# Attention into a two-layer product on one core: chunks of 512 tokens that follow the batches, with the left-over tokens gathered into a ninth

## The chip, the core and the metric

One Trainium2 chip, one core of it. The metric is device microseconds of one execution of the whole program, the median of the runs shown. Engines are named as in the profile: PE (TensorE, its weight loads apart as PEld), DVE (VectorE), ACT (ScalarE), POOL (GpSimd) and SP (SyncE, which here only issues DMAs). Each engine takes its instructions strictly in the order of its own queue.

## The reference

Eight batches of 576 tokens, 8 heads of 64. Keys and values are averaged over windows of 8 tokens, so a batch has 72 keys; attention over them gives 4,608 tokens of 512 values, which go through two matrices with a gelu between.

```python
k_p = k.reshape(B, H, Sp, pool, D).mean(axis=3)          # B=8, H=8, S=576, D=64, Sp=72
v_p = v.reshape(B, H, Sp, pool, D).mean(axis=3)
scores = scale * np.matmul(q, k_p.transpose(0, 1, 3, 2))
attn = softmax(scores)
attn_out = np.matmul(attn, v_p).astype(np.float32)
x = attn_out.transpose(0, 2, 1, 3).reshape(B * S, H * D)  # 4608 x 512
h = x @ w_in                                              # 512 x 2048
g = h * (1.0 / (1.0 + np.exp(-1.702 * h)))
out = (g @ w_out).astype(np.float32)                      # 2048 x 512
```

The two weight matrices come as float64.

## The kernel before

**Precision.** Every operand of a large product is split into a rounded part and the exact rest (`hi`, `lo`), and each product is three passes on PE: hi·hi, hi·lo, lo·hi. ACT usually makes the `hi` by a copy and DVE or POOL the `lo` by a subtraction.

**Weights.** They are decoded from float64 in 33 parts (`decode_weights`): ACT scales (L520, L522), DVE puts sign and exponent together (L527, L528), POOL adds (L532), ACT rounds to `hi` (L538), and POOL, or DVE for every fourth part, subtracts (L543). The raw words of a part lie where the part two places on will live.

**Attention.** A batch has two pieces, 256 and 320 tokens. Keys and values are loaded by SP, 64 keys of two heads to a tile, in one buffer that is refilled after DVE's window sum (L147); ACT and PE turn the keys; `score` (L308) gives scores in PSUM, DVE subtracts the maximum (L320, L321), ACT takes the exponential, DVE sums and multiplies (`tail` L381, `main` L389), turns the weights (`mt`, L422) and splits them (`al`, L426), and `weigh` (L452 to L455) makes x transposed: `pav` in PSUM, from which ACT writes `hi` (L458) and DVE `lo` (L459) of x. Batch 0's products of window sums, queries and weights are turned on PE. The work of a batch is a generator whose `yield`s give a chunk that must be through before it goes on.

**Chunks.** The second part takes the 4,608 tokens in chunks: three of 256 and ten of 384, whose borders do not match the batches. Where a piece reaches over the border of a chunk, its later tokens wait in `stage` (L461) and are moved by `unstage` (ACT L466, POOL L467). For each chunk and each 128 of the 2,048 columns (256 for a chunk of 256 tokens), `moe_in` makes h by 12 matmuls (L563 to L565), ACT makes `gh` and `g` (L569, L570), DVE (chunks 0 and 1) or POOL makes `gl` (L572); `moe_out` then adds to the chunk's output tiles of 128 tokens (L583 to L585), which stay in PSUM over the whole chunk. At the end of a chunk ACT copies each tile to `osb` (L588) and issues its DMA (L589); the first tile of a chunk borrows the one buffer of tag `g`, the others take the two of tag `osb`.

**Order.** The main loop goes through the steps (a chunk and a block of columns). Between steps it pumps the attention's generator: PACE = 5 stages a step, with EARLY = 13 ahead, as far as x has a free buffer of two. DECODED = 0.8 parts of weights are decoded per pumped stage. SP's loads stand where the program issues them: `fetch_batch(b + 1)` in piece 0 of batch b. Within these data dependencies a scheduler of the compiler puts each engine's queue in order, so the queue can differ from the program's order.

PSUM: three banks for output tiles (`ps_o`), two for h (`ps_h`), three for attention (`ps_a`).

## Time and profile before

| | |
|---|---|
| runs | 1000.5, 997.71, 998.65 us; median 998.65 |
| span of the profiled execution | 994.9 us; its own device time is not listed, and 3.75 us of the median lie outside this span |
| first product of chunk 0, of the third chunk (token 512) | 41.8 us, 185.5 us |
| first product of the last chunk | 920.8 us |
| last matmul ends | 990.3 us |
| DMA bytes | 47.2 MB read, 9.4 MB written |

Busy time is each engine's own, over the whole span; PE's large share comes from the second part, and the first 200 us look different from the rest. In rows of the profile the third and later columns of a group are busy time, mean ns of one instruction, and the engine's idle time ahead of it with what ended it.

### The profile page before, as it was taken

What the parts mean: (1) busy time and instruction counts of PE and PEld (TensorE: products, weight loads), DVE (VectorE), ACT (ScalarE), POOL (GpSimd) and SP (SyncE); (2) the same over time, 40 slices, a digit from 0 to 9 for tenths busy, and PEclk for the clock granted to TensorE, in tenths of its full rate; (3) what the DMA queues carried; (4) which work ended last, traced back from release to release, by engine and by line L of the source; (5) the groups of instructions that cost most, each with busy time, mean ns of one, the idle gap of its engine ahead of it and who ended that gap; (6) DMA issues with size and microseconds to landing.
All of it is one profiled execution on the core that took longest, in us unless ns stands there. A gap on an engine that the chain in (4) does not pass through costs nothing.

```text
span 994.9 us, 13412 instructions
## 1 busy us (share of the span) xinstructions
PE 939.4 (94%) x4957; PEld 835.0 (84%) x4957; DVE 551.3 (55%) x1094; ACT 411.9 (41%) x837; POOL 266.7 (27%) x240
## 2 busy tenths in 40 slices
PE   5597899989999999999989999999999999999998
PEld 4476698888878999899978989889988999999997
DVE  3999995789989660760788560680685410100000
ACT  3788553444336432452434342442445332322222
POOL 2568620111212222222212222222212322222222
PEclk8689799999999999999999999999999999999999
DMA  8984341312233030130223030130010000000000
GB/s 208 340 241 126 74 102 32 77 35 52 71 54 85 32 70 1 43 75 1 60 42 85 32 69 1 38 70 1 33 27 1 33 1 0 33 1 1 33 1 32
DMA packets 100449, 57.50 MB, mean 58 GB/s; under 512 B 75168, under 2 KB 83360, under 8 KB 100384
## 3 DMA queue, kind: packets, MB, share of 16 engines
q1 hardware_dynamic: 95200, 47.21, 19.6%
q10 hardware_dynamic: 5184, 9.44, 2.6%
q8 instruction: 39, 0.64, 0.3%
q14 instruction: 26, 0.21, 0.1%
HBM read 47.19 MB, written 9.44 MB: 57 GB/s over the span
## 4 chain that ended last, share of the span: by engine, by line
PE 63%; DVE 18%; DMA 6%; issue 4%; ACT 4%; SPq 3%; POOL 1%; DVEq 0%; ACTq 0%; POOLq 0%
PE h L565 10%; PE o L585 10%; PE h L564 10%; PE o L583 10%; PE h L563 10%; PE o L584 10%; DVE main L389 7%; DMA qr<-in_q_dram 2%; PE sps L308 2%; DMA tl<-in_v_dram 1%; DMA raw<-in_moe_w_out_dram 1%; SPq L183 1%; DVE al L426 1%; DVE tail L381 1%; DVE red_k L147 1%
## 5 line engine op out<-in xcount | busy, mean ns | idle before, releaser
L572 POOL TENSOR_TENSOR gl<-g,gh 128x384 fp32r<-128x384 f32 (+1 forms) x168 | 176.0, 1047 | 619.1 <-ACT g L570 595.6
L564 PE MATMUL h<-x,w 128*128 128x384 f32 (+1 forms) x832 | 274.0, 329 | 4.1 <-POOL w L543 3.5
L565 PE MATMUL h<-x,w 128*128 128x384 f32 (+1 forms) x832 | 273.5, 329 | 1.4 <-DVE x L459 1.4
L563 PE MATMUL h<-x,w 128*128 128x384 f32 (+1 forms) x832 | 273.6, 329 | 0.5 <-ACT x L458 0.4
L569 ACT ACTIVATE gh<-h 128x384 fp32r<-128x384 f32 (+1 forms) x184 | 93.0, 505 | 337.6 <-PE h L565 333.8
L583 PE MATMUL o<-w,gh 128*128 128x512 f32 x576 | 227.9, 396 | 2.6 <-ACT gh L569 2.5
L584 PE MATMUL o<-w,gh 128*128 128x512 f32 x576 | 227.8, 395 | 0.0
L585 PE MATMUL o<-w,gl 128*128 128x512 f32 x576 | 192.0, 399 | 3.3 <-DVE gl L572 3.0
L564 PEld LDWEIGHTS h<-x,w 128*128 128x128 f32 x832 | 160.2, 193 | 14.0 <-POOL w L543 4.1
L563 PEld LDWEIGHTS h<-x,w 128*128 128x128 f32 x832 | 159.9, 192 | 10.8 <-issue 0.8
L565 PEld LDWEIGHTS h<-x,w 128*128 128x128 f32 x832 | 159.2, 192 | 8.0 <-DVE x L459 1.6
L426 DVE TENSOR_TENSOR al<-mt,ah 128x256 fp32r<-128x256 f32 (+1 forms) x56 | 31.9, 569 | 180.1 <-PE pav L454 142.6
L583 PEld LDWEIGHTS o<-w,gh 128*128 128x128 f32 x576 | 108.7, 189 | 19.6 <-ACT gh L569 3.8
L585 PEld LDWEIGHTS o<-w,gl 128*128 128x128 f32 x576 | 106.2, 189 | 22.4 <-DVE gl L572 3.6
L584 PEld LDWEIGHTS o<-w,gh 128*128 128x128 f32 x576 | 108.8, 189 | 16.5 <-issue 0.4
L389 DVE TENSOR_TENSOR main<-sc,sm 32x256 f32<-32x256 f32 (+1 forms) x224 | 118.5, 529 | 3.2
L570 ACT ACTIVATE g<-h 128x384 f32<-128x384 f32 (+1 forms) x184 | 92.1, 501 | 13.8 <-DVE gl L572 6.9
L459 DVE TENSOR_TENSOR x<-pav,x 128x256 fp32r<-128x256 f32 (+3 forms) x64 | 24.9, 390 | 68.0 <-ACT x L458 67.9
L308 PE MATMUL sps<-k,qt 128*128 128x144 f32 (+1 forms) x320 | 57.6, 305 | 2.8 <-DVE sc L321 2.7
L308 PEld LDWEIGHTS sps<-k,qt 128*128 128x128 f32 (+1 forms) x320 | 45.4, 187 | 10.9 <-DVE sc L321 2.9
L532 POOL TENSOR_TENSOR raw<-raw 128x512 uint32<-128x512 uint32 (+1 forms) x33 | 41.5, 1261 | 40.8 <-DVE raw L528 14.5
L425 ACT CAST ah<-mt 128x256 fp32r<-128x256 f32 (+1 forms) x56 | 24.3, 434 | 52.9 <-DVE mt L422 39.6
(80 smaller groups left out, 891.7 us busy)
## 6 DMA issues: line engine op xcount, KB each, us to landing
out_dram<-osb ACTq DMA_DIRECT2D x36, 256.0 KB
raw<-in_moe_w_in_dram SPq DMA_DIRECT2D x16, 512.0 KB
raw<-in_moe_w_out_dram SPq DMA_DIRECT2D x15, 512.0 KB
kv_False<-in_k_dram SPq DMA_DIRECT2D x28, 256.0 KB
kv_True<-in_v_dram SPq DMA_DIRECT2D x28, 256.0 KB
qr<-in_q_dram SPq DMA_DIRECT2D x112, 40.0 KB
qr<-in_q_dram SPq DMA_DIRECT2D x112, 32.0 KB
tl<-in_v_dram SPq DMA_DIRECT2D x48, 64.0 KB
```

The lines of the kernel that those rows point to most:

```text
L308: nc.tensor.matmul(ps[:ns, t * PW : (t + 1) * PW], lhsT=qt[:, s0 - o0 : s0 - o0 + ns], rhs=m.k2[:, j], start=True, stop=True,)
L389: nc.vector.tensor_tensor(out=main[32 * r : 32 * (r + 1), :, cols].rearrange("p j t k -> p t j k"), in0=sc[rows, 0:nt, a::2, 32 * half : 3 ...
L426: nc.vector.tensor_tensor(out=al[:, :npc], in0=pt[:, :npc], in1=ah[:, :npc].bitcast(F32), op=ALU.subtract)
L563: nc.tensor.matmul(o, lhsT=w[:, 0, j], rhs=x[:, 0, j], start=j == 0, stop=False)
L564: nc.tensor.matmul(o, lhsT=w[:, 1, j], rhs=x[:, 0, j], start=False, stop=False)
L565: nc.tensor.matmul(o, lhsT=w[:, 0, j], rhs=x[:, 1, j], start=False, stop=j == NJ - 1)
L569: nc.scalar.activation(out=gh, in_=h, func=AF.Gelu_apprx_sigmoid)
L570: nc.scalar.activation(out=g, in_=h, func=AF.Gelu_apprx_sigmoid)
L572: (nc.vector if c < 2 else nc.gpsimd).tensor_tensor(out=gl, in0=g, in1=gh.bitcast(F32), op=ALU.subtract)
L583: nc.tensor.matmul(o, lhsT=gh[:, i, tok], rhs=w[:, 0], start=f == 0, stop=False)
L584: nc.tensor.matmul(o, lhsT=gh[:, i, tok], rhs=w[:, 1], start=False, stop=False)
L585: nc.tensor.matmul(o, lhsT=gl[:, i, tok], rhs=w[:, 0], start=False, stop=f == NF - 1)
```

## The change

- Chunks are of 512 tokens, one per batch: its first 512 tokens. Chunk 0 is done in two halves of 256 tokens whose steps alternate, the second half three steps behind (LAG). Chunks 1 to 7 take 16 steps of 512 tokens each.
- The last 64 tokens of each batch are copied by ACT to `left` and stored by SP to a buffer in DRAM (128 KB a batch). When chunk 6 is through, the 512 left-over tokens are loaded back (1 MB), split by ACT and DVE, and make a ninth chunk, whose output leaves in eight DMAs of 64 rows. `stage` and `unstage` are gone.
- PSUM: four banks for output tiles, two for h, two for attention; batch 0's sums use `ps_h`, queries and scores of its second piece `ps_o`.
- The first tile and the third of a chunk's output take the one buffer of tag `g`, the second and fourth the two of tag `osb`.
- Pumping goes by a table of stages that must be through at each chunk (THROUGH), spread evenly over the chunk's steps, three steps early (SOONER). DECODED goes from 0.8 to 0.3. Batch 1 is fetched, and its keys summed and turned, after all of batch 0's attention; before, they were prefetched from inside it.
- `gl` is on DVE for chunk 0 alone, which is the same 512 tokens as before.
- The raw words of the last three parts of the weights lie in the second x buffer, and batch 0's keys and values in one x buffer instead of two.

```diff
-    HEAD = 3
-    CHUNK = 384
-    OVER = 192  # tokens of a piece beyond its first chunk, at most
+    CHUNK = 512
+    HALF = CHUNK // 2
+    LEFT = S - CHUNK
     AHEAD = 1
-    PACE = 5
-    EARLY = 13
+    SOONER = 3
+    THROUGH = [53, 108] + [123 + 57 * i for i in range(1, B)]
     FETCHED = 1
-    DECODED = 0.8
+    DECODED = 0.3
+    LAG = 3
...
-    ps_o = ctx.enter_context(tc.tile_pool(name="ps_o", bufs=3, space=PSUM))
+    ps_o = ctx.enter_context(tc.tile_pool(name="ps_o", bufs=4, space=PSUM))
-    ps_a = ctx.enter_context(tc.tile_pool(name="ps_a", bufs=3, space=PSUM))
+    ps_a = ctx.enter_context(tc.tile_pool(name="ps_a", bufs=2, space=PSUM))
+    left_dram = tc.dram_tile([P, NJ, CHUNK], F32, name="left_dram")
...
-            if b + 1 < B:
+            if 0 < b < B - 1:
                 fetch_batch(b + 1)
             yield -1
-        elif b + 1 < B:
+        elif 0 < b < B - 1:
             yield from sum_keys(b + 1)
             yield from turn_keys(b + 1)
...
+            cols = slice(piece * HALF, (piece + 1) * HALF)
+            xh, xl = (x_tile(b)[:, i, j, cols] for i in range(2))
+            nc.scalar.copy(out=xh, in_=pa[:, :HALF])
+            nc.vector.tensor_tensor(out=xl, in0=pa[:, :HALF], in1=xh.bitcast(F32), op=ALU.subtract)
+            if npc > HALF:
+                nc.scalar.copy(out=left[:, j], in_=pa[:, HALF:npc])
...
+        written[0] += 1
+        if npc > HALF:
+            nc.sync.dma_start(out=left_dram[:, :, b * LEFT : (b + 1) * LEFT], in_=left)
+            if b == B - 1:
+                yield b - 1
+                x = x_tile(B)
+                nc.sync.dma_start(out=x[:, 1].bitcast(F32), in_=left_dram)
+                for j in range(NJ):
+                    nc.scalar.copy(out=x[:, 0, j], in_=x[:, 1, j].bitcast(F32))
+                    nc.vector.tensor_tensor(
+                        out=x[:, 1, j], in0=x[:, 1, j].bitcast(F32), in1=x[:, 0, j].bitcast(F32), op=ALU.subtract
+                    )
+                written[0] += 2
...
-        (nc.vector if c < 2 else nc.gpsimd).tensor_tensor(out=gl, in0=g, in1=gh.bitcast(F32), op=ALU.subtract)
+        (nc.vector if c < 1 else nc.gpsimd).tensor_tensor(out=gl, in0=g, in1=gh.bitcast(F32), op=ALU.subtract)
...
-                osb = moe.tile([P, DM], F32, tag="g" if t == t0 else "osb", name=f"osb{t}", bufs=1 if t == t0 else 2)
+                first = t % (2 * P) == 0
+                osb = moe.tile([P, DM], F32, tag="g" if first else "osb", name=f"osb{c}_{t}", bufs=1 if first else 2)
                 nc.scalar.copy(out=osb, in_=o)
-                nc.scalar.dma_start(out=out[t : t + P], in_=osb)
+                if c < B:
+                    nc.scalar.dma_start(out=out[c * S + t : c * S + t + P], in_=osb)
+                else:
+                    rows = out.rearrange("(b s) d -> b s d", s=S)
+                    for i in range(P // LEFT):
+                        nc.scalar.dma_start(
+                            out=rows[t // LEFT + i, CHUNK:], in_=osb[i * LEFT : (i + 1) * LEFT]
+                        )
...
-                if b < 2:
+                if b < 2 or (b, piece) == (2, 0):
                     yield from front
+                if b == 1 and piece == 0:
+                    fetch_batch(1)
+                    yield from sum_keys(1)
+                    yield from turn_keys(1)
...
+    halves = [[(0, o0, HALF, (f, f + 1)) for f in range(0, NF, 2)] for o0 in (0, HALF)]
+    steps = halves[0][:LAG]
+    for i in range(len(halves[1])):
+        steps += halves[1][i : i + 1] + halves[0][LAG + i : LAG + i + 1]
+    steps += [(c, 0, CHUNK, (f,)) for c in range(1, B + 1) for f in range(NF)]
+
+    def due(step):
+        c, i = divmod(step + SOONER, NF) if step + SOONER >= NF else (0, step)
+        return THROUGH[c] + (THROUGH[c + 1] - THROUGH[c]) * i // (NF if c else NF - SOONER) if c < B - 1 else math.inf
+
+    for step, (c, o0, n, fs) in enumerate(steps):
+        while written[0] < 2 * c + 2:
             pump()
...
-        while need is not None and need <= through and pumped - first < (step + 1) * PACE + EARLY:
+        while need is not None and need <= through and pumped < due(step + 1):
             pump()
```

The names in the following rows: a tile's name is followed by its batch, piece or chunk and block (`pav1_1_0` is batch 1, piece 1, block 0; `h1_0_0` is chunk 1; before, `h512_0` is named by its first token). The first two pieces show PE's queue where the products of the tokens from 512 on come near. Before, the weighted sums of batch 1's first piece stand among the products of the second chunk:

```order
L583 MATMUL o384_1497<-w1_9_521,gh256_8_1701 128x512
L584 MATMUL o384_1497<-w1_9_521,gh256_8_1701 128x512
L452 MATMUL pav1_0_2_1351<-ah1_0_2_1347,vh1_1242 128x256
L453 MATMUL pav1_0_2_1351<-ah1_0_2_1347,vl1_1243 128x256
L585 MATMUL o384_1497<-w1_9_521,gl256_8_1702 128x512
L563 MATMUL h256_12_1813<-x1_887,w0_12_656 128x256
L564 MATMUL h256_12_1813<-x1_887,w0_12_656 128x256
L454 MATMUL pav1_0_2_1351<-al1_0_2_1348,vh1_1242 128x256
```

and in the changed kernel the last products of chunk 0 and what follows them:

```order
L586 MATMUL o0_384_1044<-w1_15_1531,gh0_256_14_1943 128x512
L587 MATMUL o0_384_1044<-w1_15_1531,gh0_256_14_1943 128x512
L588 MATMUL o0_384_1044<-w1_15_1531,gl0_256_14_1944 128x512
L452 MATMUL pav1_1_0_1733<-ah1_1_0_1685,vh1_1067 128x320
L453 MATMUL pav1_1_0_1733<-ah1_1_0_1685,vl1_1068 128x320
L454 MATMUL pav1_1_0_1733<-al1_1_0_1686,vh1_1067 128x320
L455 MATMUL pav1_1_0_1733<-at1_1_0_1675,vt1_1071 128x320
L452 MATMUL pav1_1_1_1747<-ah1_1_1_1743,vh1_1067 128x320
L453 MATMUL pav1_1_1_1747<-ah1_1_1_1743,vl1_1068 128x320
L566 MATMUL h1_0_0_1970<-x1_1158,w0_0_179 128x512
```

Before, `pav` of piece 0 lies between products of the chunk in front; now those of batch 1's piece 1 stand behind the last product of chunk 0. DVE at that place in the changed kernel, a few rows behind `gl0_256_14`, the split of the last `g` of chunk 0, and ahead of the first `al` of piece 1:

```order
L146 TENSOR_REDUCE red2_v1_2076<-kv2_1_True_1658 128x128
L381 TENSOR_TENSOR tail1_1_1490<-sc1_1_1271,sm1_1_1273 32x2x32 x2
L381 TENSOR_TENSOR tail1_1_1490<-sc1_1_1271,sm1_1_1273 32x3x32 x2
L389 TENSOR_TENSOR main1_1_1489<-sc1_1_1271,sm1_1_1273 32x3x4x32 x4
L381 TENSOR_TENSOR tail1_1_1490<-sc1_1_1271,sm1_1_1273 32x3x32 x2
L389 TENSOR_TENSOR main1_1_1489<-sc1_1_1271,sm1_1_1273 32x3x4x32 x4
L389 TENSOR_TENSOR main1_1_1489<-sc1_1_1271,sm1_1_1273 32x2x4x32 x4
L381 TENSOR_TENSOR tail1_1_1490<-sc1_1_1271,sm1_1_1273 32x2x32 x2
L389 TENSOR_TENSOR main1_1_1489<-sc1_1_1271,sm1_1_1273 32x2x4x32 x4
L149 TENSOR_TENSOR vbd2_2072<-red2_v1_2076,mask2_84 128x256
L437 STREAM_TRANSPOSE tt1_1_1673<-tail1_1_1490 64x320
L146 TENSOR_REDUCE red3_k0_2445<-kv3_0_False_2086 128x128
```

In before, piece 0 of batch 1 at the same place has the `gl` of the running chunk in between:

```order
L572 TENSOR_TENSOR gl256_4_1549<-g256_4_1547,gh256_4_1548 128x512
L147 TENSOR_REDUCE red2_v0_2099<-kv2_0_True_1663 128x128
L445 TENSOR_TENSOR at1_0_0_1309<-tt1_0_1307,at1_0_0_1309 32x256
L445 TENSOR_TENSOR at1_0_1_1313<-tt1_0_1307,at1_0_1_1313 32x256
L572 TENSOR_TENSOR gl256_6_1622<-g256_6_1620,gh256_6_1621 128x512
L422 STREAM_TRANSPOSE mt1_0_0_1317<-main1_0_1119 128x256
L426 TENSOR_TENSOR al1_0_0_1320<-mt1_0_0_1317,ah1_0_0_1319 128x256
```

So DVE's attention of batch 1 ran under chunk 1's products before, and the multiplications of its second piece now stand behind chunk 0's last `gl`. SP's queue, in before where batch 1's keys are first loaded:

```order
L504 DMA raw18_368<-in_moe_w_in_dram 128x4x256
L504 DMA raw19_390<-in_moe_w_out_dram 128x1024
L504 DMA raw20_411<-in_moe_w_in_dram 128x4x256
L98 DMA kv1_0_False_429<-in_k_dram 64x2x512 x2
L114 DMA tl1_0_435<-in_v_dram 32x1x512 x3
```

and in the changed kernel:

```order
L508 DMA raws_469<-in_moe_w_out_dram 128x512
L129 DMA qr1_0_0_749<-in_q_dram 32x8x32
L129 DMA qr1_0_1_754<-in_q_dram 32x8x32 x4
L129 DMA qr1_0_2_764<-in_q_dram 32x8x32 x4
L129 DMA qr1_0_3_771<-in_q_dram 32x8x32 x4
L475 DMA left_dram_92<-left0_1_566 512x1x64
L97 DMA kv1_0_False_662<-in_k_dram 64x2x512 x2
```

The load of batch 1's keys stood among the weights' loads and now stands behind the store of batch 0's left-over tokens. ACT's last rows before:

```order
L588 COPY osb4224_9060<-o4224_8653 128x512
L588 COPY osb4352_9066<-o4352_8657 128x512
L588 COPY osb4480_9072<-o4480_8661 128x512
L589 DMA out_0_dram<-osb4224_9060 128x512
L589 DMA out_0_dram<-osb4352_9066 128x512
L589 DMA out_0_dram<-osb4480_9072 128x512
```

and now:

```order
L592 COPY osb8_0_8195<-o8_0_7742 128x512
L592 COPY osb8_128_8202<-o8_128_7746 128x512
L598 DMA out_0_dram<-osb8_0_8195 64x512 x2
L598 DMA out_0_dram<-osb8_128_8202 64x512 x2
L592 COPY osb8_256_8209<-o8_256_7750 128x512
L592 COPY osb8_384_8216<-o8_384_7754 128x512
L598 DMA out_0_dram<-osb8_256_8209 64x512 x2
L598 DMA out_0_dram<-osb8_384_8216 64x512 x2
```

Three copies and three DMAs have become two copies, four DMAs, two copies and four DMAs, and the third copy writes to the buffer that the first two DMAs read.

More of the change, by code (lines that the diff above doesn't have):

```diff
@@ L272, in attention @@
         npc = sum(c for _, c in tiles)
-        t0 = b * S + o0
-        first = next(c for c, (c0, w) in enumerate(CHUNKS) if t0 < c0 + w)
-        inside = min(npc, sum(CHUNKS[first]) - t0)
         whole = [t for t, (_, c) in enumerate(tiles) if c == P]
@@ L305, in score @@
         def score(j, qt):
-            ps = ps_a.tile([P, 512], F32, tag="a", name=f"sps{n}_{j}")
+            if whole_q and piece:
+                ps = ps_o.tile([P, DM], F32, tag="o", name=f"sps{n}_{j}")
+            else:
+                ps = ps_a.tile([P, 512], F32, tag="a", name=f"sps{n}_{j}")
             for t, (s0, ns) in enumerate(tiles):
@@ L455, in weigh @@
             nc.tensor.matmul(o, lhsT=m.vt[:96, j], rhs=at[:96, :npc], start=False, stop=True)
[L456 to L477 removed]
+            cols = slice(piece * HALF, (piece + 1) * HALF)
[5 more added lines that the diff above has]
+        if npc > HALF:
+            left = att.tile([P, NJ, LEFT], F32, tag="left", name=f"left{n}")
         ats, parts = tail_parts(), None
@@ L639, in pump @@
             more_weights(int(pumped * DECODED))
-    steps = []
-    for c, (t0, n) in enumerate(CHUNKS):
-        nf = max(512 // n, 1)
-        steps += [(c, t0, n, tuple(range(f, f + nf))) for f in range(0, NF, nf)]
-    for step, (c, t0, n, fs) in enumerate(steps):
-        while written[0] < t0 + n:
-            pump()
-        if step == 0:
-            first = pumped
-        more_weights(2 * fs[-1] + 2 + (fs[-1] == NF - 1) + (LEAD if t0 == 0 else 0))
-        pending.append((t0, n, fs, *moe_in(t0, n, fs)))
-        if fs[-1] == NF - 1:
+    halves = [[(0, o0, HALF, (f, f + 1)) for f in range(0, NF, 2)] for o0 in (0, HALF)]
[8 more added lines that the diff above has]
+        while written[0] < 2 * c + 2:
+            pump()
+        more_weights(2 * fs[-1] + 2 + (fs[-1] == NF - 1) + (LEAD if c == 0 else 0))
+        pending.append((c, o0, n, fs, *moe_in(c, o0, n, fs)))
+        if fs[-1] == NF - 1 and o0 + n == CHUNK:
             through = c
```

76 lines of the change are left out of this document (28 added, 48 removed).

## The prediction

> **What bounds the kernel now.** I read the page first, then busy time by stretches of the span, the timeline of TensorE (PE) at a few places, the groups by shape, and the last microseconds. The page says that PE is the engine to watch:
>
> ```profile
> span 994.9 us, 13412 instructions
> PE 939.4 (94%) x4957; PEld 835.0 (84%) x4957; DVE 551.3 (55%) x1094; ACT 411.9 (41%) x837; POOL 266.7 (27%) x240
> PE   5597899989999999999989999999999999999998
> DVE  3999995789989660760788560680685410100000
> ```
>
> The mean hides two kernels. The stretches (columns: length, then busy time of PE, PEld, DVE, ACT, POOL with instruction counts, then granted PE clock, DMA share, GB/s) show them:
>
> ```profile
> 0.00:25.00 25.00, 12.57 (x62) 10.66 (x62) 9.30 (x20) 7.85 (x15) 5.32 (x10) 0.86 0.81 209
> 25.00:50.00 25.00, 12.92 (x64) 10.28 (x64) 24.71 (x39) 19.90 (x39) 14.59 (x12) 0.69 1.03 340
> 150.00:175.00 25.00, 23.45 (x147) 20.84 (x148) 14.77 (x31) 9.25 (x23) 0.00 (x0) 1.00 0.13 34
> 200.00:250.00 50.00, 46.70 (x278) 41.27 (x277) 45.51 (x99) 24.09 (x42) 8.23 (x7) 0.97 0.22 44
> 250.00:300.00 50.00, 45.93 (x242) 39.95 (x241) 45.20 (x97) 19.45 (x44) 9.36 (x9) 1.00 0.27 61
> 500.00:600.00 100.00, 97.00 (x503) 86.20 (x503) 70.38 (x150) 43.51 (x92) 22.23 (x21) 1.00 0.25 57
> 700.00:800.00 100.00, 98.52 (x520) 88.60 (x519) 66.74 (x147) 43.78 (x97) 22.27 (x22) 1.00 0.09 23
> ...
> 0.00:150.00 150.00, 112.62 (x609) 94.64 (x609) 132.90 (x216) 96.54 (x177) 82.06 (x65) 0.85 0.65 181
> 150.00:185.50 35.50, 33.95 (x208) 29.55 (x209) 20.67 (x47) 12.99 (x30) 0.96 (x1) 1.00 0.17 38
> ```
>
> For the first 150 us VectorE (DVE) is busy 132.9, and 15.7 of its 17.1 idle us lie in the first 25: DVE, decoding weights and doing two batches' attention, sets the pace. Between 150 and 185.5 it is busy only 20.7 of 35.5: it and PE wait for each other. Later PE is near 100%, except where attention crowds together: 3.3 us idle in 200 to 250, 4.1 in 250 to 300, 3.0 in 500 to 600, 1.5 in 700 to 800, 11.9 together.
>
> How fast PE goes when nothing holds it is the distance from start to start:
>
> ```profile
> 174.26 0.28 PE L565 MATMUL h<-x,w 128*128 128x256 f32 x1
> 174.38 0.39 PE L583 MATMUL o<-w,gh 128*128 128x512 f32 x1
> ...
> 175.98 0.39 PE L584 MATMUL o<-w,gh 128*128 128x512 f32 x1
> ...
> 185.48 0.28 PE L563 MATMUL h<-x,w 128*128 128x256 f32 x1
> ...
> 854.05 0.34 PE L563 MATMUL h<-x,w 128*128 128x384 f32 x1
> ...
> 856.13 0.39 PE L583 MATMUL o<-w,gh 128*128 128x512 f32 x1
> 856.36 0.39 PE L584 MATMUL o<-w,gh 128*128 128x512 f32 x1
> ```
>
> A matmul of 256 columns takes 0.12 us (174.26 to 174.38), one of 384 takes 0.1733 (12 from 854.05 to 856.13), one of 512 takes 0.229 to 0.230 (7 in 1.60; 856.13 to 856.36). I use 0.12, 0.1734 and 0.2295. The row at 185.48 is the first product of token 512, the point at which I cut the span.
>
> **The sum, step by step.** It is made as a difference to the profiled execution: span 994.9, against a median of 998.65 for the runs, so 3.75 us lie outside the span, and I leave them as they are.
>
> *PE's own work.* First products before: 3 chunks x 192 matmuls x 0.12 + 10 x 192 x 0.1734 = 69.1 + 332.9 = 402.0. After: 384 x 0.12 + 8 x 192 x 0.2295 = 46.1 + 352.5 = 398.6. The second products stay at 1,728. So -3.4 us; with 0.2286 or 0.23 for 512 columns it is -4.8 or -2.6. The Trainium skill, TensorE: Matmul & The Clock Gate, section "Wait — 56ns, not 53.3ns?", has a full-speed matmul cost its columns plus a fixed 2.5 ns or so; by that, 576 matmuls fewer would save only an estimated 1.4 us, while the rows here give more.
>
> *The start.* This is the large term. After, chunk 1 (tokens 512 on in the new order) needs both pieces of batch 1, where before chunk x2 needed only piece 0. So DVE must do more before it. I counted what stands ahead of the last write of chunk 1's x on DVE against what before had done by 150 us; nothing of the latter is missing, and the extra items are 46.6 us by these groups and the small ones:
>
> ```profile
> L147 DVE TENSOR_REDUCE red_v<-kv_True 128x128 f32<-128x1024 f32 x14 | 27.9, 1992 | 0.1
> L147 DVE TENSOR_REDUCE red_k<-kv_False 128x128 f32<-128x1024 f32 x14 | 27.8, 1984 | 5.0 <-DMA kv_False<-in_k_dram 5.0
> L389 DVE TENSOR_TENSOR main<-sc,sm 32x256 f32<-32x256 f32 x168 | 81.0, 482 | 2.3
> L389 DVE TENSOR_TENSOR main<-sc,sm 32x384 f32<-32x384 f32 x56 | 37.5, 669 | 0.9
> L572 DVE TENSOR_TENSOR gl<-g,gh 128x512 fp32r<-128x512 f32 x16 | 13.3, 833 | 4.3 <-ACT g L570 4.2
> L426 DVE TENSOR_TENSOR al<-mt,ah 128x256 fp32r<-128x256 f32 x28 | 16.3, 584 | 97.5 <-PE pav L454 92.3 <-ACT ah L425 4.8
> L381 DVE TENSOR_TENSOR tail<-sc,sm 32x64 f32<-32x64 f32 x84 | 24.1, 286 | 1.4
> L381 DVE TENSOR_TENSOR tail<-sc,sm 32x96 f32<-32x96 f32 x28 | 10.1, 362 | 0.4
> ```
>
> At those means, 3 window sums are 6.0, 18 `main` multiplications 10 x 0.482 + 8 x 0.669 = 10.2, 7 `gl` 5.8, 8 `tail` 2.6, 8 `al` 4.7: 29.3. Some forty small instructions (transposes, score reductions, `at`, `x`) make the rest, and as Pool is idle then and DVE's two-operand forms run shorter I use the median of each form, which gives 46.6 for all. If DVE stayed as busy as in before's first 150 us, chunk 1 would be complete at 150 + 46.6 = 196.6. That is the lower end.
>
> Two waits come on top. First, batch 1's keys were fetched early in before; after, their load stands behind the store of the left-over tokens on SyncE's (SP's) queue, and the next thing but two on DVE is their sum. Each such load takes as long as here:
>
> ```profile
> 268.65 2.01 DVE L147 TENSOR_REDUCE red_v<-kv_True 128x128 f32<-128x1024 f32 x1
> ...
> 275.53 1.98 DVE L147 TENSOR_REDUCE red_k<-kv_False 128x128 f32<-128x1024 f32 x1 [0.72 <-DMA kv_False<-in_k_dram]
> ...
> 270.69 1.25 SPq L98 DMA_DIRECT2D kv_False<-in_k_dram  x2
> ```
>
> A sum ends at 270.66, the buffer's next load is issued at 270.69, and its data are there at 275.53: 4.9 us, of which DVE had other work for all but 0.72. After, nine such loads follow each other at this distance ahead of chunk 1, at six of them with only 2 to 4 us of DVE work between: by subtracting row by row, some 10 us of waits. Second, DVE's score reductions of batch 1 alternate with PE's score matmuls, which stand behind chunk 0's products: about 10.7 us more if none overlaps (before shows the pattern: 14.8 us idle in 150 to 185.5). Together 0 to 20.7; I take four fifths, 16.4, since both are written into the queues' order, and less than all since one wait can cover part of the other. So chunk 1 is complete, and begins in earnest, at 213 (197 to 217).
>
> There is a second way to see it. Behind `gl0_256_14`, which PE needs 8 matmuls (1.8 us) before chunk 0 ends, DVE has 16 `main`, 8 `tail`, two window sums and some dozen others to do before `al1_1_0`, by the rows above 15 to 20 us, and PE has nothing else queued: PE stands still for about 14 to 18 us.
>
> What this costs: 213 - 185.5 = 27.5, less the attention work that PE has then done earlier than before (piece 1 of batch 1 and keys of batch 2, 9.2 us at the paces above): +18.3 (+1.9 to +22.3). By the same page's section "What's actually happening", an idle window of some 3.4 us drops PE to half clock for about as long again, an estimated 1.7 us more that is not in the sum; before's stretch at 25 to 50 has a clock of 0.69, with PE half idle, so the trace bears that out as far as it goes.
>
> *The rest of the stream.* From 185.5 to PE's last end at 990.3 are 804.8 us. Its work there: 45.0 (chunk x2) + 10 x (33.3 + 33.0) + 69.2 of attention = 777.5. So before loses 27 there, 11.9 outright idle and the rest in thin spots. After, with attention spread evenly by step and each chunk holding one batch, I give 6 for one small wait a chunk, and 5 for chunk borders. At a border two output tiles now share one buffer, `g`'s, so the third tile's copy and then the next `g` wait for a DMA that takes 3.2 us here:
>
> ```profile
> 789.23 0.34 ACTq L589 DMA_DIRECT2D out_dram<-osb  x1
> ...
> 792.78 0.49 ACT L570 ACTIVATE g<-h 128x384 f32<-128x384 f32 x1 [0.43 <-DMA out_dram<-osb]
> ```
>
> Two h buffers cover most of that (0.2 to 0.5 left at each of five borders, 1.4 to 4 where the ninth chunk is loaded from DRAM behind chunk 6). So 11 (8 to 20) in place of 27: -16. The copies to `left`, the eight stores and Pool's lost `unstage` lie on engines that are idle over half of the span: nothing, but if ScalarE (ACT) were late at a border they would be part of the 20. `gl` on Pool goes from 1.03 to 1.37 us a step:
>
> ```profile
> L572 POOL TENSOR_TENSOR gl<-g,gh 128x512 fp32r<-128x512 f32 x8 | 10.9, 1366 | 48.9 <-ACT g L570 48.9
> ...
> L585 PE MATMUL o<-w,gl 128*128 128x512 f32 x576 | 192.0, 399 | 3.3 <-DVE gl L572 3.0 <-POOL gl L572 0.3
> ```
>
> With `gh` and `g` ahead of it that is 2.6 us, under the 5.5 of PE's step of 24 matmuls of 512 columns: nothing; uncovered, it would be 0.3 in each of 128 steps, and PE's waits for Pool's `gl` are 0.3 in all now. One bank fewer for scores and weighted sums makes PE's scores wait sooner for DVE's reading of them; that is in the 10.7.
>
> *The end.* Before:
>
> ```profile
> 989.44 0.85 PE L585 MATMUL o<-w,gl 128*128 128x512 f32 x3
> 989.87 1.07 ACT L588 COPY osb<-o 128x512 f32<-128x512 f32 x2 [2.79 <-PE o L585]
> 990.83 0.60 ACT L588 COPY osb<-o 128x512 f32<-128x512 f32 x1
> 990.97 0.85 ACTq L589 DMA_DIRECT2D out_dram<-osb  x2
> ```
>
> From 990.29 to 994.9 are 4.6 us, the last 3.1 from the last issue's end to the landing. After, the third tile's copy waits for the first tile's two DMAs: copies 0.5, issues to 1.3, landing 4.4, two copies to 5.0 or so, four issues at 0.49 to 6.9, landing 10.0: +5.4.
>
> Sum: -3.4 + 18.3 - 16 + 5.4 = +4.3. So 998.65 + 4.3 = 1003.
>
> **Rivals.** *The start costs little* (faster). If the loads of batch 1 and 2 and PE's scores arrive while DVE has other work, as before's 1.4 us of idle time in 25 to 150 speaks for, chunk 1 is complete at about 199: start +4.3, the rest as above: -3.4 + 4.3 - 16 + 5.4 = -9.7, 989. Against it: the load behind the store, and DVE's queue behind `gl0_256_14`. It decides at 209: earlier than that, and the sum is below zero.
>
> *The borders bite* (slower). Third tile's copy, `g` and ACT's in-order queue hold PE 1.5 us or more at each of eight borders, and chunk 1 begins at 217: later losses 20 in place of 11, start +22.3: +15, 1014. For it: `g` waits 0.43 us for a DMA even now, with one tile in its buffer; against it: PE has a chunk's last second products, 2.8 us, to do meanwhile.
>
> *Pacing does not pace* (slower). Steps are paced in program order, but a scheduler then orders each queue; if attention still crowds, the 27 us stay: -3.4 + 18.3 + 0 + 5.4 = +20, 1019. Against it: even now four chunks of ten hold nearly all the idle time.
>
> **How the numbers follow.** My forecast (997 to 1008) has 0.4, the cheap start 0.3, the borders 0.2, the pacing 0.1. This kernel's time can be told from no change at about 0.3%, 3 us: 995.7 to 1001.6. The forecast's own range lies partly in it: 0.22 of its 0.4, the rest above. A little of the cheap start falls in it as well. So faster 0.29, same 0.23, slower 0.48. The range takes in the cheap start's value with its lower end, and the borders' value: 985 to 1018. The forecast's own range is 997 to 1008.
>
> **What would show it.** Right: the first product of chunk 1 near 213, with a PE stall of 14 us or so just ahead, ended by DVE's `al`; DVE waits on `kv` DMAs and on `sps` between 150 and 200; no stall over 2 us later, except at the border into chunk 7 or 8; 10 us from the last matmul to the end. Wrong: chunk 1 before 205, or stalls of some us in every chunk after it.

## The result, and the profile after

The changed kernel takes 1025.05 us (four runs, 1023.21 to 1026.51) against 999.22 before: 1.0253 times as long, with a 95% interval of 1.0236 to 1.027. The forecast was 1003, at most 1018. The side was right, the size was not: +26 instead of +4. The profiled execution spans 1023.3 us (its own time is 1025.0). Its page:

```profile
span 1023.3 us, 12057 instructions
PE 934.2 (91%) x4381; PEld 766.8 (75%) x4381; DVE 556.9 (54%) x1098; ACT 398.0 (39%) x747; POOL 241.3 (24%) x192
PE   5466897939999989999999999999999999999996
DVE  3999778487876793767376737674636100000000
PEclk9579699969999999999999999999999999999999
```

PE's row is all nines from the tenth slice on, but for an 8 in the fifteenth (358 to 384 us) and the last slice: between 384 us and the end hardly anything is lost. DVE's row no longer has, behind 400 us, the peaks of 8 that it had before. Nearly all that went wrong lies in the first 384 us. Busy time by stretches, up to where batch 1 and batch 2 have their x complete, first of the changed kernel (complete at 236.2 and 339.6), with the rest of the stream as a third row:

```profile
0.00:236.20 236.20, 163.84 (x872) 137.33 (x873) 182.54 (x313) 116.59 (x221) 73.26 (x64) 0.83 0.46 127
0.00:339.60 339.60, 265.99 (x1348) 220.61 (x1349) 264.34 (x488) 160.28 (x302) 94.15 (x80) 0.88 0.38 100
400.00:1014.50 614.50, 613.24 (x2784) 502.78 (x2782) 248.09 (x525) 211.71 (x401) 135.20 (x103) 1.00 0.13 33
```

and of the kernel before (complete at 236.1 and 302.5):

```profile
0.00:236.10 236.10, 193.87 (x1111) 166.52 (x1112) 198.37 (x361) 132.25 (x247) 91.08 (x72) 0.90 0.49 131
0.00:302.50 302.50, 256.19 (x1441) 220.56 (x1442) 259.65 (x492) 162.38 (x308) 103.45 (x83) 0.92 0.45 117
```

Batch 1 is complete at the same time in both, but PE has then been busy 30 us less (163.84 against 193.87), and DVE 16 us less. Batch 2 is complete 37 us later, at nearly the same DVE work (264.34 against 259.65): DVE stood idle 75.3 us until then, before 42.9.

A second measure is used below. PE's *lag* is the time at which a chunk's first `gh` starts, less the work that PE's queue holds ahead of it at the paces of the prediction. It rises where PE waits or is slow. It is an estimate, good to some 2 us, since the attention's narrow matmuls have no settled pace:

| point | before | changed |
|---|---|---|
| chunk 0 | 39.3 (at 62.0 us) | 50.3 (at 77.2) |
| token 512 on | 62.2 (190.1) | 102.0 (237.0) |
| about 340 us | 75.9 (333.9) | 105.8 (342.1) |
| about 440 us | 77.4 (445.1) | 112.5 (442.5) |
| last matmul ends | 88.8 (990.3) | 116.5 (1014.5) |
| end of the span | 4.6 us later | 8.8 us later |

So the difference of the spans, 28.4, is -3.5 of work, +39.8 up to token 512, -12.1 behind it and +4.2 at the end. (The medians differ by 25.8. The changed kernel's profiled time is 1.7 us longer than its span, where the prediction kept 3.75 for before.) Of the 39.8, 11.0 are there already when chunk 0 makes its first `gh`, at 77.2 us instead of 62.0. PE's waits from 77 to 236 us, changed kernel:

```profile
PE pav L452 <- ACT ah L425: 15.2, 2, 15.0
PE o L588 <- DVE gl L575: 10.1, 5, 3.7
PE h L566 <- ACT x L458: 3.8, 2, 3.3
PE h L568 <- DVE x L459: 3.8, 2, 3.1
```

and before, in the same stretch, the two longest:

```profile
PE h L564 <- POOL w L543: 3.5, 2, 1.9
PE o L585 <- DVE gl L572: 3.0, 1, 3.0
```

The first row is the stall that the order had shown, behind the last product of chunk 0. Here it is on PE's timeline, and the matmuls after it:

```profile
209.95 0.40 PE L588 MATMUL o<-w,gl 128*128 128x512 f32 x1
225.38 0.64 PE L452 MATMUL pav<-ah,vh 128*128 128x320 f32 x1 [15.04 <-ACT ah L425]
...
227.72 0.63 PE L566 MATMUL h<-x,w 128*128 128x512 f32 x1
228.15 0.63 PE L567 MATMUL h<-x,w 128*128 128x512 f32 x1
228.57 0.63 PE L566 MATMUL h<-x,w 128*128 128x512 f32 x1
...
233.52 0.40 PE L567 MATMUL h<-x,w 128*128 128x512 f32 x1
233.76 0.39 PE L566 MATMUL h<-x,w 128*128 128x512 f32 x1
```

The row at 227.72 is the first product of chunk 1. From 225.4 to 231.1 a matmul of 512 columns takes 0.42 us (228.15 to 228.57), then 0.24 or less: the stall is followed by 5.7 us at half pace, 2.8 us lost. The granted clock is 0.50 from 225.4 to 231.1 us and 0.99 in the 6 us behind. On DVE in that stall, almost without a gap (some rows left out):

```profile
207.48 0.69 DVE L575 TENSOR_TENSOR gl<-g,gh 128x512 fp32r<-128x512 f32 x1 [0.89 <-ACT g L573]
...
211.63 2.23 DVE L389 TENSOR_TENSOR main<-sc,sm 32x384 f32<-32x384 f32 x4
...
214.40 3.95 DVE L389 TENSOR_TENSOR main<-sc,sm 32x384 f32<-32x384 f32 x8
...
225.36 0.49 DVE L426 TENSOR_TENSOR al<-mt,ah 128x320 fp32r<-128x320 f32 x1 [0.53 <-ACT ah L425]
```

It is 17.9 us from the last `gl` of chunk 0 to the first `al` of piece 1, and PE had 2.9 us of work for it. What DVE itself waited for, 112 to 242 us, longest groups:

```profile
DVE red_k L146 <- DMA kv_False<-in_k_dram: 6.4, 4, 3.0
DVE al L426 <- PE pav L454: 4.8, 3, 1.8
DVE al L426 <- ACT ah L425: 4.4, 5, 2.1
DVE red_v L146 <- DMA kv_True<-in_v_dram: 4.2, 2, 2.5
DVE gl L575 <- ACT g L573: 3.6, 3, 2.4
DVE nm L320 <- PE sps L308: 3.1, 2, 2.7
DVE qt L293 <- PE sps L308: 2.4, 2, 2.1
DVE vl L254 <- ACT vh L253: 2.3, 1, 2.3
DVE sm L359 <- ACT sc L354: 2.1, 1, 2.1
DVE w L547 <- ACT w L542: 1.4, 1, 1.4
```

Loads make 10.6, waits for PE 10.3, and waits for ACT 14.0 (with one of 0.2 that is not shown). PE and ACT wait for DVE in turn.

### The profile page after: what moved, and what is told of

The parts are those of the page before. It is cut to its first block, busy times and chain, and to the rows that moved or that the text cites. A ratio compares the mean times of both kernels' runs of the same rounds, so it can differ in the third digit from the quotient of the medians.

```text
span 1023.3 us, 12057 instructions
## 1 busy us (share of the span) xinstructions
PE 934.2 (91%) x4381; PEld 766.8 (75%) x4381; DVE 556.9 (54%) x1098; ACT 398.0 (39%) x747; POOL 241.3 (24%) x192
## 4 chain that ended last, share of the span: by engine, by line
PE 63%; DVE 16%; DMA 10%; issue 4%; SPq 3%; ACT 3%; POOL 0%; DVEq 0%; ACTq 0%; POOLq 0%
PE h L566 10%; PE o L588 10%; PE o L586 10%; PE o L587 10%; PE h L568 10%; PE h L567 10%; DVE main L389 5%; DMA kv_False<-in_k_dram 3%; PE sps L308 2%; DMA raw<-in_moe_w_in_dram 2%; DMA qr<-in_q_dram 1%; DVE red_k L146 1%; DMA kv_True<-in_v_dram 1%; DVE raw L532 1%; SPq L97 1%
## 5 line engine op out<-in xcount | busy, mean ns | idle before, releaser
L575 POOL TENSOR_TENSOR gl<-g,gh 128x512 fp32r<-128x512 f32 x128 | 168.1, 1313 | 683.1 <-ACT g L573 646.4
L566 PE MATMUL h<-x,w 128*128 128x512 f32 (+1 forms) x640 | 244.8, 383 | 7.8 <-ACT x L458 5.9
L568 PE MATMUL h<-x,w 128*128 128x512 f32 (+1 forms) x640 | 239.1, 376 | 3.9 <-DVE x L459 3.8
L567 PE MATMUL h<-x,w 128*128 128x512 f32 (+1 forms) x640 | 239.5, 374 | 0.0
L588 PE MATMUL o<-w,gl 128*128 128x512 f32 x576 | 209.5, 397 | 11.7 <-DVE gl L575 10.1
L572 ACT ACTIVATE gh<-h 128x512 fp32r<-128x512 f32 x144 | 86.2, 599 | 321.9 <-PE h L568 312.7
L566 PEld LDWEIGHTS h<-x,w 128*128 128x128 f32 x640 | 123.8, 193 | 33.1 <-ACT x L458 7.0
L568 PEld LDWEIGHTS h<-x,w 128*128 128x128 f32 x640 | 123.0, 193 | 25.8 <-DVE x L459 4.8
L567 PEld LDWEIGHTS h<-x,w 128*128 128x128 f32 x640 | 123.8, 193 | 19.8 <-issue 0.4
L389 DVE TENSOR_TENSOR main<-sc,sm 32x256 f32<-32x256 f32 (+1 forms) x224 | 114.9, 513 | 3.2
L573 ACT ACTIVATE g<-h 128x512 f32<-128x512 f32 x144 | 85.4, 593 | 35.7 <-DMA out_dram<-osb 23.2
L320 DVE TENSOR_REDUCE nm<-sps 128x4 f32<-128x288 f32 (+1 forms) x96 | 36.7, 386 | 58.2 <-PE sps L308 58.1
L426 DVE TENSOR_TENSOR al<-mt,ah 128x256 fp32r<-128x256 f32 (+1 forms) x56 | 28.5, 510 | 51.7 <-ACT ah L425 46.3
L536 POOL TENSOR_TENSOR raw<-raw 128x512 uint32<-128x512 uint32 x30 | 35.4, 1180 | 41.1 <-DVE raw L532 23.6
```

The costliest lines, as they stand in the source:

```text
L320: nc.vector.tensor_reduce(out=nm[:ns, g, hs], in_=pv, axis=AX.X, op=ALU.max, negate=True)
L389: nc.vector.tensor_tensor(out=main[32 * r : 32 * (r + 1), :, cols].rearrange("p j t k -> p t j k"), in0=sc[rows, 0:nt, a::2, 32 * half : 3 ...
L566: nc.tensor.matmul(o, lhsT=w[:, 0, j], rhs=x[:, 0, j], start=j == 0, stop=False)
L567: nc.tensor.matmul(o, lhsT=w[:, 1, j], rhs=x[:, 0, j], start=False, stop=False)
L568: nc.tensor.matmul(o, lhsT=w[:, 0, j], rhs=x[:, 1, j], start=False, stop=j == NJ - 1)
L572: nc.scalar.activation(out=gh, in_=h, func=AF.Gelu_apprx_sigmoid)
```

## The experiments

My first theory (D) was that the loss comes of one dependency: chunk 1 needs the second piece of batch 1, and PE has nothing else. Its rivals were the loads (L) and the turn-taking halves of chunk 0 (I). All times below are medians; the changed kernel has 1025.05, and the kernel before 999.2 to 1000.7 beside them. Ratios are to the kernel before, with the 95% interval.

**Chunk 1 in two halves** (all of chunk 1's steps of 256 tokens, first half first):

```diff
-    steps += [(c, 0, CHUNK, (f,)) for c in range(1, B + 1) for f in range(NF)]
+    steps += [(1, o0, HALF, (f, f + 1)) for o0 in (0, HALF) for f in range(0, NF, 2)]
+    steps += [(c, 0, CHUNK, (f,)) for c in range(2, B + 1) for f in range(NF)]
...
-        while written[0] < 2 * c + 2:
+        while written[0] < 2 * c + (1 if c == 1 and o0 == 0 else 2):
```

> Chunk 1 in two halves of 256, the first of which needs only batch 1's first piece; all else as in the changed kernel. Theory D (PE runs dry because chunk 1 needs the second piece of batch 1, which DVE reaches at 236 us): the stall of 15.4 us at 210 goes, and so does part of the thin stretch to 236; with 2 us more for matmuls of 256 columns, about 1005 us (1000 to 1012), first product of chunk 1 ahead of 215. Rivals L (waits for loads of keys and values) and I (the two halves of chunk 0 taking turns delay PE from the start): the loss lies ahead of 200 us already, PE only moves the stall to the second half; 1018 to 1027.

1022.7 us (1019.65 and 1025.77), 1.0236 (1.0162 to 1.031). Its two runs lie 6 us apart, so the time can't be told from the changed kernel's. The stall of 15 us is gone, as D said: the lag at chunk 1's first `gh` is 82.9 instead of 102.0. But it is 98.4 at chunk 2 and 108.8 at the end, where the changed kernel has 105.8 and 116.5: batch 2 is complete at 334 us instead of 340, and PE waits there for its x (2.5 us at 334, for DVE). D explains where PE stood, not why DVE was late; as the cause of the whole loss it falls.

**Chunk 0's halves one after the other** (LAG = 8):

> Chunk 0's halves one after the other instead of taking turns (LAG 8). Rival I: the first half's products are out sooner, PE's lag behind its own work at the first product of the second half falls from 66 to near 58 us, and 8 to 12 us of that last to the end: 1013 to 1017. Theory D: chunk 1 still needs both pieces of batch 1, DVE's work ahead of it is the same 183 us; within 4 us of the changed kernel, 1021 to 1029.

1027.7, 1.0286 (1.0257 to 1.0316): 2.7 more. Rival I falls.

**No loads of keys and values** behind the first (`fetch_main` returns one shared tile; all later window sums read that one):

> Leaves out all loads of keys and values behind the first of batch 1: the sums of all later ones read that one tile. Rival L: DVE's waits for these loads, 10.6 us ahead of chunk 1 and some 24 in all, go, and the time falls by 10 or more: 1010 to 1015. Theory D: part of the 10.6 turns into waits for PE's scores, which stand in order with chunk 0's products; 3 to 8 us less: 1017 to 1022.

1015.4, 1.0163 (1.0134 to 1.0193): 9.7 less, as L said. The loads' waits are gone from DVE's list, yet only 3.2 us were gained up to chunk 1 (lag 98.8 for 102.0): over the whole span DVE's waits for scores grew instead, from

```profile
DVE nm L320 <- PE sps L308: 58.1, 17, 5.8
```

to

```profile
DVE nm L325 <- PE sps L313: 82.3, 23, 6.9
```

**Half tiles of keys and values in three buffers**, all loads kept (the reduction is done in two halves):

```diff
-            t = load.tile([P, NP, 512], F32, tag="kv", name=f"kv{b}_{u}_{src is v}")
+            t = []
+            for i in range(NP):
+                t.append(load.tile([P, 512], F32, tag="kv", name=f"kv{b}_{u}_{src is v}_{i}", bufs=3))
```

> Keys and values loaded in half tiles with three buffers in place of whole tiles with one; nothing left out. Theory L: as the run without loads, DVE's waits on these loads go; 6 to 10 us less than the changed kernel, 1015 to 1019. If the loads are late because SP's queue holds them behind other loads and stores, not for want of a buffer: within 3 us, 1022 to 1026.

1019.95, 1.0198 (1.0168 to 1.0227): 5 less. A real remedy returns half of what leaving the loads out does.

**Three buffers for the other output tiles**, `first = t == 0` (the decoding's `e`, of the same tag, gets three buffers with them):

> Only the first tile of a chunk borrows the buffer of g; the three others have three buffers of their own. The term for the end (8.8 us behind the last matmul against 4.6 before) should fall to 5.5 to 6.5, and waits at chunk borders for the output's DMA should go: 4 to 6 us less if those waits count, 1019 to 1021; 2 to 3 less, 1022 to 1023, if the borders are covered.

1022.4, 1.0234 (1.0204 to 1.0263). The 2.6 us less is what was expected if the borders are covered. The end is still 8.5 us: in the changed kernel the third copy waits 2.6 us for the first two DMAs, as predicted, but without that wait nothing is won, since ACT now stands in the issues themselves:

```profile
1011.70 3.19 ACTq L598 DMA_DIRECT2D out_dram<-osb  x5
1014.99 0.59 ACT L592 COPY osb<-o 128x512 f32<-128x512 f32 x1 [2.92 <-issue]
```

**The old pumping rule in the changed kernel** (`pumped < 53 + 13 + 5 * (step + 1)`):

> The changed kernel with the old pumping rule put back (five stages a step, 13 ahead) in place of the even table. Theory P (the even table brings batch 2's attention too late: complete at 340 us against 302.5 before, so the 10 us of PE's lag added around the start of chunk 2 are its price): batch 2 is complete by 320 or earlier and 6 to 12 us come back, 1013 to 1019. Rival G (even pacing is what saves the later losses, as the prediction had it): attention crowds at each chunk's front again, later losses go from 14.5 back toward 27, 1031 to 1038.

1039.3, 1.0391 (1.0357 to 1.0426): 14 more. Theory P falls, rival G holds (a us above its range), and the table is worth 14 us here: with the old rule the lag goes from 106.7 at chunk 1 to 132.2, with the table from 102.0 to 116.5, so that 11 of the 14 come behind chunk 1's start. Batch 2 is not sooner by it (344.5 us).

**Chunk 1 in halves, half tiles in three buffers, SOONER = 8** together:

> Chunk 1 in two halves, half tiles of keys and values in three buffers, and the even table taken eight steps early instead of three. If the loss is a chain of DVE's attention of batches 1 and 2 (theory D with L and P): the stall ahead of chunk 1 and the one ahead of chunk 2 both go, PE's lag at its last matmul falls from 116.5 to 95 (90 to 100), 1003 (998 to 1008). If the three act on the same wait: as the best of them alone, 1014 to 1018.

1018.7, 1.0185 (1.0155 to 1.0214). The lag at chunk 1 is 77.1, at chunk 2 95.4, at the end 107.5: the lags at chunks 1 and 2 fall, and the waits behind them take most of the gain, so that the time is hardly better than with half tiles alone.

**Three stages a step in the kernel before** (PACE = 3):

> The kernel before with three stages a step in place of five, all else the same. If even pacing by itself gives back later losses (the prediction's second term): 6 to 13 us less than before, 986 to 993. If attention is late by it, as theory P has it for the changed kernel: 1000 to 1010. If the scheduler's order does not follow the pumping: within 3 us of 999.

1013.7, 1.0135 (1.0106 to 1.0165): batch 2 comes at 347 instead of 302.5 us. It starves the early part and tells nothing of the later one.

So the question became why DVE does the same work 37 us later. One run puts the whole early order back, three put back parts of it.

**The whole early part as before** (chunks 0 and 1 in halves one after the other, DECODED = 0.8, batch 1 fetched inside batch 0, no draining ahead of batch 2, the old pumping rule through chunk 1):

```diff
-    DECODED = 0.3
+    DECODED = 0.8
...
-    LAG = 3
+    LAG = 8
...
-            if 0 < b < B - 1:
+            if b < B - 1:
                 fetch_batch(b + 1)
             yield -1
-        elif 0 < b < B - 1:
+        elif b < B - 1:
...
-                if b < 2 or (b, piece) == (2, 0):
+                if b < 2:
                     yield from front
-                if b == 1 and piece == 0:
-                    fetch_batch(1)
-                    yield from sum_keys(1)
-                    yield from turn_keys(1)
...
-    steps += [(c, 0, CHUNK, (f,)) for c in range(1, B + 1) for f in range(NF)]
+    steps += [(1, o0, HALF, (f, f + 1)) for o0 in (0, HALF) for f in range(0, NF, 2)]
+    steps += [(c, 0, CHUNK, (f,)) for c in range(2, B + 1) for f in range(NF)]
...
-        while written[0] < 2 * c + 2:
+        while written[0] < 2 * c + (1 if c == 1 and o0 == 0 else 2):
...
-        while need is not None and need <= through and pumped < due(step + 1):
+        while need is not None and need <= through and pumped < (53 + 13 + 5 * (step + 1) if step < 32 else due(step + 1)):
```

> The changed kernel with the whole early part put back as it was before: chunks 0 and 1 in halves one after the other, weights decoded at 0.8 parts a stage, batch 1 fetched and its keys summed inside batch 0, the old pumping rule through chunk 1, the even table from chunk 2. Theory E (the loss is DVE's idle time until batch 2 is complete, 75 us against 43 before, and the early order makes it): DVE's idle time by then falls below 55, batch 2 is complete by 315, PE's lag at the end is 85 to 98, 993 to 1006. Rival B (it is the banks: two for scores instead of three, or the ninth chunk and the border chains): the early order gains nothing over the version with chunk 1 in halves, 1015 to 1023.

1006.55, 1.0067 (1.0047 to 1.0088): 18.5 less, the largest gain of all, yet not all of it. At token 512 the lag is 65.5, near the 62.2 of before; at chunk 2 it is 91.1. DVE still does less by its time than before did:

```profile
0.00:327.00 327.00, 265.19 (x1545) 229.24 (x1545) 255.21 (x486) 161.31 (x303) 95.91 (x80) 0.90 0.40 106
```

DVE is idle 71.8 us until batch 2 is complete, at 327. So the early order is shown to make 18.5 us of the loss, but not in the way of theory E, which had this idle time below 55 and batch 2 by 315: the idle time hardly moved from 75.3. What changed is that PE has done its 265 us of work by 327 us, in the changed kernel only by 340. DVE's idle time by itself is no measure of the loss.

**Parts of it alone.** The decoding rate:

> Only the decoding rate put back, 0.8 parts of weights a pumped stage for 0.3. If slow decoding starves chunk 0 (last decode at 158 us against 127 before): 5 to 12 us less than the changed kernel, 1013 to 1020. If DVE is simply full, its work only changes places: 1021 to 1029.

1024.6, 1.0245 (1.0194 to 1.0296): nothing. The early fetch of batch 1:

> Only the prefetch of batch 1 put back: its loads, key sums and turning inside batch 0's attention. Theory L (loads behind the store): the first wait of 3.0 us goes and perhaps the next, 2 to 5 us less, 1020 to 1023. If summing keys early delays batch 0's second piece, which chunk 0's second half needs: 1026 to 1033.

1016.8, 1.0168 (1.0128 to 1.0207): 8 less, more than the first wait of 3.0 us; batch 1 is complete at 226.7 instead of 236.2. The halves of chunks 0 and 1 in sequence:

> Chunk 1 in halves and chunk 0's halves one after the other, nothing else put back. Theory E with the order of the halves as its main part: 1005 to 1012. If the halves of chunk 0 don't matter, as their run alone said: as chunk 1 in halves alone, 1018 to 1025.

1022.5, 1.0225 (1.0175 to 1.0274): no more than chunk 1 in halves alone. Of the 18.5, the fetch gives 8 when alone, the halves some 2, which is within the scatter; the rest needs them together, or comes of the draining or of the pumping rule through chunk 1, which were not tried alone (the old rule throughout costs 14).

**Chunk 2 in halves as well**, on top of the early part as before:

> The version with the early part as before, and chunk 2 in two halves as well. Theory E (each chunk up to the one of batch 2 waits for the whole of a batch that DVE has not done): the stall of some 15 us ahead of chunk 2 goes, 2 us more for matmuls of 256 columns, PE's lag at the end is 82 to 88, 990 to 997. Rival (the stall only moves to the next chunk, since DVE stays behind): lag 93 to 97, 1003 to 1008.

1011.2, 1.0127 (1.0105 to 1.0149): 4.6 more, not 13 less. PE does start chunk 2 at a lag of 84.0, but stands at 93.8 at its second half: the wait only moves. Theory E in the form that the grain of a whole batch is the cause falls here.

**The lost bank**, alone, in the kernel before (`ps_a` with two banks for three):

> The kernel before with two PSUM banks for attention in place of three, all else the same. If the lost bank is what keeps DVE waiting for scores (rival B): 6 to 15 us more than before, 1005 to 1015, and DVE's idle time until batch 2 is complete rises from 43 to over 55. If two banks do: within 3 us of 999.5.

1006.8, 1.0083 (1.0057 to 1.0109): 7.5 more than before, by one constant. Until batch 2 is complete, at 330.0 us:

```profile
0.00:330.00 330.00, 277.09 (x1536) 237.11 (x1537) 263.71 (x487) 166.00 (x317) 105.52 (x88) 0.92 0.40 107
```

DVE stands idle 66.3 us there instead of 42.9, and chunk 0's first `gh` comes at 67.6 us instead of 62.0. So the lost bank costs 7.5 us in the old order. What it costs in the changed kernel is not shown: no run gave it a third bank for attention. The early part as before still lacks it, and may owe its last 7 us to it; that its 1006.55 is so near the 1006.8 here proves nothing, since the two differ in much else.

**Both the lost bank and the late fetch** in the kernel before:

> The kernel before with two banks for attention and batch 1 fetched, summed and turned only after all of batch 0's attention, as in the changed kernel; chunks, pumping and the rest as before. If the lost bank (7.5 us alone in the kernel before) and the late loads (8 us, from the changed kernel with the early fetch) add up: 1012 to 1019, DVE's idle time until batch 2 is complete over 72 us. If they are the same wait: 1005 to 1010.

1005.8, 1.0058 (1.0036 to 1.008). They don't add up: the late fetch costs nothing more here. A reason may be that with chunks of 256 tokens PE has other products to do while batch 1's keys come late; no run shows it.

**A version faster than both?** The early part as before, chunk 2 in halves, half tiles, and the ninth chunk's third tile in a buffer of `gh`:

> As the former, with half tiles of keys and values in three buffers and, in the ninth chunk alone, the third tile's copy in a buffer of gh. The end shortens from 8.8 to 5.5 or so, and DVE's waits for loads go: 4 to 8 us less than the former, 985 to 992, faster than the kernel before. If the loads no longer count once the early part is as before: 3 us less than the former.

1007.9, 1.0098 (1.0077 to 1.0118): 3 less than the former, as the second reading had it. The end is 8.2 us, not 5.5. And even pacing alone in the kernel before, from step 39 on (`ahead = min(ahead, 233 + int(2.2 * (step - 38)))`), then the same with 2.8:

> The kernel before, with its old rule until step 39 (batch 3 begun, attention a chunk ahead) and from there 2.2 stages a step instead of bursts of 29 or 57. If even pacing by itself gives back later losses (PE's lag grows by 13 us from 76 behind that point now): 5 to 10 us less than before, 989 to 995. If the bursts are cheap because the scheduler spreads them anyway: within 3 us of 999.

> The same at 2.8 stages a step, a smaller step from the bursts. If what counts is that each chunk's attention is spread: most of the same gain, 990 to 996. If 2.2 was already short of what some chunk needs: faster than 2.2 by 2 to 4 us.

999.4 and 999.4, 0.9994 (0.9983 to 1.0005) and 0.9994 (0.9984 to 1.0003): no change. PE's largest wait from 400 to 900 us is the same with 2.2 as before, first the one, then before:

```profile
PEld pav L454 <- DVE al L426: 5.4, 4, 1.8
```

```profile
PEld pav L454 <- DVE al L426: 5.5, 4, 1.9
```

A reason may be that x has two buffers, so that x of a chunk can't be written until the chunk two before it is through, whatever the pace of the stages; no run varied that. No version here beats the kernel before.

## Why the prediction was wrong

**PE's work, -3.4: right.** The ninth chunk, with no attention beside it, takes 82.1 us from its first `gh` to its last (926.9 to 1009.0), where the paces give 82.6.

**The start, +18.3: wrong, the failed step.** The step read that chunk 1 "is complete, and begins in earnest, at 213 (197 to 217)"; it was complete at 236.2, outside its own bounds, with the first product at 227.7. Two of its parts held: DVE's work was 182.5 us for a forecast 179.5 (132.9 and 46.6), and the stall 15 for "14 to 18". What failed is the list of DVE's waits. It had two entries, loads ("some 10") and PE's scores ("about 10.7 us more if none overlaps"), of which four fifths were taken. From 115 us to 236.2 DVE stood idle 35.4: 10.6 for loads, 10.3 for PE (the scores and `pav`), and 14.0 for ACT (`ah`, `g`, `vh`, `sc`, `w`), which the step had put at nothing. So both entries came in full, and the missing one was the largest. The forecast had 33.5 us of idle time in all (17.1 and 16.4), the run 53.7; with 3.0 more of work that is the whole of the 23 us. The waits of before in the stretch that the step called the pattern, 150 to 185.5, had shown it, 7.3 for ACT and 6.5 for PE:

```profile
DVE gl L572 <- ACT g L570: 4.2, 4, 1.4
DVE al L426 <- ACT ah L425: 3.1, 2, 2.6
DVE qt L296 <- PE sps L308: 2.8, 1, 2.8
DVE nm L320 <- PE sps L308: 2.1, 1, 2.1
DVE al L426 <- PE pav L454: 1.6, 1, 1.6
```

I had also put the lost bank into the 10.7 in one sentence without a price; alone it costs 7.5 us in the kernel before, and how much of the waits above it makes is not shown. Nor had the step a term for chunk 0's later start (11.0 of the lag); but the early part as before starts chunk 0 at 78.7 us too and is near before's lag at token 512, so that this delay need not last. PE's half pace behind the stall, 2.8 us, was left out of the sum (an estimated 1.7 in the prediction). The Trainium skill, TensorE: Matmul & The Clock Gate, section "What's actually happening", has full clock come back after some 3.4 us of sustained work; here it took 5.7, with short waits of PE in between.

**The rest of the stream, -16: the sign right, the size 12.1.** Before lost 26.6 from token 512 on, for a forecast 27; the changed kernel 14.5, for a forecast 11. By the table 3.8 of it come in chunk 1, 6.7 in chunk 2, and 4.0 from chunk 3 to the end, where small waits and borders together stay well below the 11 that were priced. Chunk 2 does not wait for batch 2, which is complete at 339.6, just ahead of it. PE's waits from 342 to 443 us are

```profile
PE pav L454 <- DVE al L426: 2.7, 1, 2.7
PE h L566 <- ACT g L573: 1.6, 2, 1.0
PE o L588 <- POOL gl L575: 1.1, 1, 1.1
```

The first is for batch 3, on DVE. The second is, at least in part, the border that the prediction described: at 352 us ACT's `g` had waited 4.1 us for the output's DMA. That the table is worth something is shown by the run with the old rule, 14 us slower. In the old chunks even pacing by itself gained nothing, in two runs.

**The end, +5.4: size nearly right (+4.2), reason wrong.** The wait for the shared buffer is there, but two runs without it end in 8.5 and 8.2 us instead of 8.8; see below.

**The rivals.** "Pacing does not pace" came nearest in size (1019), by luck: the run with the old rule shows that the table does pace. "The borders bite" (1014) had chunk 1 at 217 and the rest of its loss at the borders, where little of it was. None named the cause.

What stays open: how much of the 18.5 us of the early order is the pumping rule, the draining, and the halves together with the early fetch; what the lost bank costs in the changed kernel; and why DVE idles 72 us with the early part as before but 66 with two banks in the kernel before.

## What to carry to other kernels

When an engine is given more to do ahead of a deadline, list its waits for every engine that feeds it, from a stretch of the trace that already has that work: here the waits for ACT, left out, were the largest. Where two engines hand tiles to and fro, count the buffers between them: one PSUM bank fewer for scores cost 7.5 us by itself, and no list of busy times of the kernel before shows it. A price for such a loop comes from a run with one buffer fewer. And a larger chunk needs more of its input complete before it can begin: ask what the fed engine has to do until then, and whether the next chunk will have the same wait.

## What the runs showed of the hardware

The last outputs leave at half the rate. Over the last microseconds, in 40 slices, the busy share of the 16 DMA engines in tenths and GB/s, of the changed kernel (DMAs of 64 partitions, 128 KB each):

```profile
DMA  0000010000000000000000589887009889930000
GB/s 0 0 0 0 0 34 0 0 0 0 0 0 0 0 0 0 0 0 0 0 0 0 129 198 216 198 203 160 0 4 211 198 198 203 211 78 0 0 0 0
```

and before (128 partitions, 256 KB):

```profile
DMA  0000000000000000000000000000007999970000
GB/s 0 0 0 0 0 0 0 0 0 0 0 0 0 0 0 0 0 0 0 0 0 0 0 0 0 0 0 0 0 0 289 382 388 371 393 273 0 0 0 0
```

198 to 216 GB/s in the full slices against 371 to 393. The DMA engines are about as busy in both, 80% and more, so it is not want of issued work that halves the rate, though ACT's issues too are longer there (0.61 us each in the median against 0.34). The 1.05 MB of the ninth chunk's output take an estimated 5 us at that rate, and neither of the two other choices of copy buffers brought the end below 8.2. The Trainium skill, SBUF — State Buffer, section "Door 1: The DMA port swizzle (why `[64,N]` ≈ `[32,N]`)", says that partitions 0 to 63 reach only half of the ports, and 64 to 127 the other half; that fits the rates if the two halves go one after the other, which no run here shows by itself.
